# A fused attention and gated-convolution kernel: the softmax exchange from tile 6, queries and keys turned in blocks from tile 7 and fetched with four tokens per partition, and a new order of the opening

## The chip, the core and the metric

The kernel runs on one core of one Trainium2 chip. A core has a matrix engine (TensorE, PE in the rows; its weight loads are PEld), a vector engine (VectorE, DVE), a scalar engine (ScalarE, ACT), a general engine (GpSimd, POOL) and a sequencer that issues DMAs (SyncE, SP). The five run side by side, each works through its own queue in order, and they wait for each other by semaphores. The metric is the time on the device in microseconds (us); shorter is better.

## The reference

Two stages, in fp32. There are 8 sequences of 576 tokens, 8 heads of 64, a model width of 512 and a hidden width of 1024.

```python
scores = q @ k.T / sqrt(64) - slope[head] * |i - j|     # masked to 0 <= i - j < 128
attn = exp(scores - max) / (sum + 1e-9)                 # over the keys
x = concat over heads of attn @ v                       # (8, 576, 512)
h = relu(x @ w_in)                                      # (8, 576, 1024)
conv_out[s] = w[0]*h[s-1] + w[1]*h[s] + w[2]*h[s+1]     # per channel, zeros outside the sequence
out = (h * sigmoid(conv_out)) @ w_out                   # (8, 576, 512)
```

## The kernel before

**Tiles, chunks, steps.** The 8 x 576 tokens are one row of 4608, cut into 36 attention tiles of 128 tokens. A query tile sees its own 128 keys and the 128 before, so both tiles' scores go into one buffer and a predicated copy chooses by position. Sequence boundaries fall at multiples of 576, that is on a tile edge at tiles 9, 18 and 27, and in the middle of tiles 4, 13, 22 and 31. The second stage works in 18 chunks of 256 tokens, each in 4 steps of 256 hidden channels: step s belongs to chunk s // 4.

**The order.** It is written by hand as strings of pieces. `OPENING` (lines 862 to 892) runs once, `PERIOD` 14 times (two tiles and four steps in each), `TAIL` once. Each piece is a letter code with a tile (or step) and sometimes a half; it issues its instructions at the end of the queues of its engines, so the string is the order on every engine at once, and pieces near each other in it are meant to run at about the same time. The pieces that matter here, by engine:

- PE: `QU` transposes queries and keys of half a tile (4 transposes; `Q` is a whole tile, 8), `S` scores, `T` transposes the softmax of half a tile (4), `AV` softmax times values, `UH` step s's up-projection (8 matmuls in fp32 for steps 0 to 3, 12 later), `D` its down-projection.
- DVE: `MP` and `MB` mask and add the bias, `TQ` block transpose of queries and keys, `TE` block transpose of the softmax, `CA`/`CB` the outer taps of the convolution, `GT` the gate, `V` the bits of a weight block, `XF` copies one column of the ring that holds the attention output x.
- ACT: `QV` copies transposed queries and keys out of PSUM, `HQ` rounds block-turned ones to the matmul's type, `X` exponentials, `Z`, `TH`, `HH`, `GH` of the second stage.
- POOL: `CL`, `SG` on weight blocks, `SEL`/`CE` cut the softmax by position, `GL` the low part of the gate.
- Either of two engines, by sets at lines 155 to 161: `W` the low part of a weight block, `LQ` the low part of queries and keys, `N` the normalising, `RS` a scaling of a weight block.
- SP: `LD`, `LV` loads of queries and keys and of values, `F` weight blocks, `WE`/`SE` the exchange, and the output.

**Two ways for queries and keys.** Matmuls contract over partitions, so queries and keys must be turned. Up to tile 8 (`t < TURN`, 9) they are loaded with one token per partition, transposed on PE and copied by ACT; tiles 7 and 8 have their low parts from `QM` and `QL` on DVE, and the keys of tile 6 are converted for tile 7 by `KH`, `KL` and `KT`. From tile 9 each DMA brings 32 tokens of 4 heads (`load_blocks`, 16 DMAs a tile), and DVE transposes in blocks of 32 by 32:

```python
nc.sync.dma_start(out=dst[:, g, (r + m) // BK],
                  in_=src[b, g * NB : (g + 1) * NB, s + m : s + m + BK, :])
```

`HQ` and `LQ` then read the block in the order in which it lies, 1024 values a partition in one instruction each.

**Two ways for the softmax.** Before tile 8 (`t < FIRST`) PE transposes it (`T`), ACT copies it (`RL`), POOL cuts it (`SEL`), and `AV` has 32 matmul records with 128 rows. From tile 8 DVE transposes blocks (`TE`), SP writes them to DRAM (`WE`) and reads them back with the blocks exchanged (`SE`), POOL cuts them (`CE`), and `AV` has 64 records with 64 rows, whose two halves are summed by `XA` (ACT) and `XS` (DVE); `XL`, the low part of x, is on POOL there and on DVE before.

**Where the stages meet.** The first up-projection in the long form, `UH4.0`, reads x of tiles 2 and 3 and one column of tile 4, which `XF4` on DVE has to put in place.

## Time and profile before

| what | value |
|---|---|
| median of 3 runs (lowest, highest) | 570.08 us (568.88, 571.22) |
| the profiled execution's own time | 568.98 us |
| its span, first to last instruction | 567.3 us |
| PE busy | 558.1 us, 98% of the span |
| DVE busy | 463.2 us, 82% |
| ACT busy | 430.6 us, 76% |
| POOL busy | 394.8 us, 70% |
| mean granted clock of PE | 0.997 |

Busy time is the time in which an engine has an instruction running, overlaps counted once. It is an average over stages with different limits, so the rows below go by stretches of the opening. Matmuls are pipelined: what a group of them costs PE is the distance from its start to the start of the next group, not the printed duration, which holds the last one's way through the array.

### The profile page before, as it was taken

The page shows a single profiled execution, that of the slowest core. Times are in us where ns is not written, and L with a number is a line of the kernel's source. Part 1 is how long each engine was busy: PE and PEld are TensorE (multiplying, and loading weights), DVE is VectorE, ACT ScalarE, POOL GpSimd, SP SyncE. Part 2 cuts the span into 40 slices and gives each one's busy share as a digit, 9 for nine tenths or more (in the row PEclk, how much of TensorE's full clock was granted, in tenths as well). Part 3 has the DMA queues.
Part 4 walks back from the last instruction along what each step waited for, and adds up shares of the span by engine and source line. Part 5 has one row for each costly group of instructions (what it writes and reads, how often), then busy time and mean ns, then how long its engine had stood idle before and what let it go on. Part 6 is the DMA issues. An engine that isn't in the chain of part 4 may idle for free.

```text
span 567.3 us, 16990 instructions
## 1 busy us (share of the span) xinstructions
PE 558.1 (98%) x6121; PEld 490.0 (86%) x6121; DVE 463.2 (82%) x1474; ACT 430.6 (76%) x1225; POOL 394.8 (70%) x453
## 2 busy tenths in 40 slices
...
GB/s 196 260 251 138 258 36 76 99 70 160 134 156 139 131 164 125 175 121 173 124 177 124 172 125 174 125 175 125 174 123 171 125 171 79 150 112 25 16 11 66
DMA packets 141225, 76.63 MB, mean 135 GB/s; under 512 B 116412, under 2 KB 131028, under 8 KB 141140
## 3 DMA queue, kind: packets, MB, share of 16 engines
...
q8 instruction: 48, 0.79, 0.6%
q14 instruction: 37, 0.30, 0.2%
...
## 4 chain that ended last, share of the span: by engine, by line
PE 91%; DVE 4%; DMA 2%; issue 1%; SPq 1%; ACT 0%; DVEq 0%
PE o L801 34%; PE p L698 34%; PE sc L387 8%; PE av L592 7%; PE o L791 2%; DMA rqk<-in_k_dram 2%; PE sc L432 2%; DVE sc L458 1%; PE av L632 1%; PE p L693 1%; SPq L320 1%; DVE wg L216 1%; PE pt L330 1%; DVE e L476 1%; DVE low L209 0%
## 5 line engine op out<-in xcount | busy, mean ns | idle before, releaser
L698 PE MATMUL p<-ring,wi 128*128 128x256 f32 x1088 | 195.4, 281 | 0.0
L731 DVE SCALAR_TENSOR_TENSOR zp<-hh,cw,zp 128x256 f32<-128x256 f32 (+7 forms) x384 | 160.5, 418 | 41.5 <-ACT zp L716 34.0
L698 PEld LDWEIGHTS p<-ring,wi 128*128 128x128 f32 x1088 | 168.7, 188 | 3.3 <-issue 0.2
L698 PE MATMUL p<-ring,wl 128*128 128x256 f32 x544 | 152.3, 280 | 0.0
L767 POOL TENSOR_TENSOR gl<-z,gh 128x512 fp32r<-128x512 f32 x67 | 86.8, 1296 | 79.9 <-ACT gh L758 79.1
L484 ACT ACTIVATE e<-e,st 128x128 f32<-128x128 f32 x288 | 112.7, 394 | 17.7 <-DVE st L476 17.4
L801 PE MATMUL o<-wo,gh 128*128 128x512 f32 x270 | 110.3, 409 | 0.0
L801 PE MATMUL o<-wo,gl 128*128 128x512 f32 x270 | 105.7, 392 | 0.0
L801 PE MATMUL o<-wl,gh 128*128 128x512 f32 x270 | 105.6, 391 | 0.0
L698 PEld LDWEIGHTS p<-ring,wl 128*128 128x128 f32 x544 | 102.7, 189 | 0.0
L716 ACT ACTIVATE zp<-hh,cw 128x256 f32<-128x256 f32 x144 | 68.9, 478 | 30.8 <-DVE z L746 20.2
L508 POOL TENSOR_TENSOR e<-e,st 128x512 f32<-128x512 f32 x60 | 62.4, 1041 | 15.1 <-DVE st L496 14.9
L368 POOL TENSOR_TENSOR qkT_low<-blk,qkT 128x1024 fp32r<-128x1024 f32 x25 | 59.9, 2397 | 16.8 <-ACT qkT L361 10.5
L476 DVE CUSTOM_DVE_ANT_0 e<-sc,bias 128x128 f32<-128x128 f32 x288 | 69.0, 285 | 1.1 <-DVE sc L458 0.2
L738 ACT ACTIVATE zp<-zp 128x512 f32<-128x512 f32 (+1 forms) x73 | 42.1, 577 | 33.3 <-DVE zp L731 33.1
L801 PEld LDWEIGHTS o<-wo,gh 128*128 128x128 f32 x270 | 50.6, 187 | 13.8 <-issue 0.2
L746 DVE SCALAR_TENSOR_TENSOR z<-zp,hh 128x512 f32<-128x512 f32 (+1 forms) x73 | 49.3, 676 | 14.1 <-ACT zp L738 12.3
L801 PEld LDWEIGHTS o<-wo,gl 128*128 128x128 f32 x270 | 50.6, 187 | 11.6
L710 ACT ACTIVATE hh<-p 128x512 f32<-128x512 f32 x67 | 40.0, 597 | 26.2 <-PE p L698 24.1
L801 PEld LDWEIGHTS o<-wl,gh 128*128 128x128 f32 x270 | 50.8, 188 | 9.5
L458 DVE COPY_PREDICATED sc<-m_prev,sc 128x256 f32<-128x256 uint8 x128 | 50.9, 420 | 8.9 <-PE sc L387 6.4
L484 ACT ACTIVATION_READ_ACCUMULATOR e<-e,st 128x1 f32 x288 | 54.3, 188 | 0.0
...
## 6 DMA issues: line engine op xcount, KB each, us to landing
...
```

What stands on the lines that cost most here:

```text
L368: eng.tensor_tensor(out=turned_of(qkT_low, t), in0=blks[t], in1=hi, op=ALU.subtract)
L387: nc.tensor.matmul(to, turned_of(tq, t)[rows, 0, g, b], of, start=n == 0, stop=n == len(passes) - 1)
L458: nc.vector.copy_predicated(out=s_cur, mask=mask.unsqueeze(1).to_broadcast(shp), data=data)
L476: nc.vector.tensor_tensor_reduce(out=e[:, j, :], in0=s_cur[:, g, :], in1=bias[:, head_of(t, u * HU + j), :], scale=-0.125, scalar=FAR, op0 ...
L484: nc.scalar.activation(out=e[:, j, :], in_=e[:, j, :], func=AF.Exp, bias=st[:, 0, j : j + 1], scale=-1.0, accum_out=st[:, 1, j : j + 1],)
L508: eng.tensor_tensor(out=e, in0=e, in1=st[:, 2, :].unsqueeze(2).to_broadcast([P, HU, P]), op=ALU.mult)
L698: nc.tensor.matmul(ps, a[:, part], ring[:, i, cc, cols], start=cc == 0 and n == 0, stop=cc == NCC - 1 and n == 2)
L716: nc.scalar.activation(out=zps[s][:, ff, :], in_=hhs[s][:, ff, 1 : 1 + CW], func=AF.Copy, scale=cw[:, 1, f : f + 1])
L731: nc.vector.scalar_tensor_tensor(out=z[:, ff, a:cut], in0=hh[:, ff, a + kk : cut + kk], scalar=cw[:, kk, f : f + 1], in1=z[:, ff, a:cut], ...
L746: nc.vector.scalar_tensor_tensor(out=zgs[s][:, ff], in0=zps[s][:, ff], scalar=1.0, in1=hhs[s][:, ff, 1 : 1 + CW], op0=ALU.add, op1=ALU.mult,)
L767: eng.tensor_tensor(out=gl, in0=zgs.pop(s), in1=as32(gh), op=ALU.subtract)
L801: nc.tensor.matmul(to, a[:, ff, ms], w[:, part], start=first and n == 0, stop=end and n == 2)
```

## The change

- `EXCH = 6`: the exchange by blocks (`TE`, `WE`, `SE`, `CE`, `AV` in quarters, `XA`, `XS`, `XL` on POOL) is used from tile 6 on instead of tile 8.
- `TURN = 7`: queries and keys are turned by blocks from tile 7 on instead of tile 9. Tile 7 also needs the keys of tile 6 in this form, so they are loaded and turned a second time, with tile 7. `QM`, `QL`, `QO`, `Q`, `KH`, `KL` and `KT` are gone; up to tile 6 the scores have one pass.
- `load_blocks`: each partition receives four tokens next to each other (1 KB) instead of one. A whole tile takes 4 DMAs (2 for queries, 2 for keys) instead of 16. A tile with a sequence boundary in its middle (13, 22, 31) takes 32 of 16 partitions each, instead of 16 of 128.
- A turned block now holds its tokens in the order of the four-token groups. `HQ` and `LQ` put them back in order as they read: the innermost dimension of the read is 4 values, 128 bytes apart. Each is now two instructions of 512 values a partition (queries, keys), and three for tile 7.
- Other engines for some pieces: `LQ9` and `LQ10` go from DVE to POOL (and `LQ7`, `LQ8` exist on POOL), `GL4` and `GL8` from POOL to DVE, one `W` and several `N` and `RS` change engine.
- `OPENING` is written anew. `PERIOD` and `TAIL` are the same strings.

The core of the diff:

```diff
+    EXCH = 6
+    TURN = 7
...
-    LOW_POOL = {2, 3, 7, 8, 9, 10, 11, 13, 14, 16}
-    RB_POOL = {0, 1, 3, 4, 5, 7, 9, 15}
-    N_ACT = {(1, 0), (2, 0), (3, 0), (4, 0), (4, 1), (5, 0), (5, 1)}
-    N_POOL = {(6, 0), (6, 1), (7, 0), (7, 1), (8, 0), (8, 1), (9, 0), (9, 1), (10, 0), (10, 1)}
-    GL_DVE = set()
-    KL_POOL = {(6, 0)}
-    LQ_DVE = {9, 10}
+    LOW_POOL = {1, 6, 7, 8, 10, 11, 12, 13, 14, 15, 16}
+    RB_POOL = {0, 3, 5, 8, 15}
+    N_ACT = {(1, 1), (2, 0), (3, 0), (4, 0), (4, 1), (5, 0), (5, 1), (7, 0), (9, 0), (9, 1)}
+    N_POOL = {(6, 0), (6, 1), (8, 0), (8, 1), (10, 0), (10, 1)}
+    GL_DVE = {4, 8}
+    LQ_DVE = set()
...
-                for m in range(0, n, BK):
-                    nc.sync.dma_start(
-                        out=dst[:, g, (r + m) // BK],
-                        in_=src[b, g * NB : (g + 1) * NB, s + m : s + m + BK, :],
-                    )
+                of = src[b, g * NB : (g + 1) * NB, s : s + n, :].rearrange("h (p m) d -> h p (m d)", m=NB)
+                if n == P:
+                    nc.sync.dma_start(out=dst[:, g].rearrange("p m d -> p (m d)"), in_=of)
+                    continue
+                for h in range(NB):
+                    rows = slice(h * BK + r // NB, h * BK + (r + n) // NB)
+                    nc.sync.dma_start(out=dst[rows, g].rearrange("p m d -> p (m d)"), in_=of[h])
...
+            if t == TURN:
+                raws[t, "k"] = apool.tile([P, NG, NB, D], F32, name=f"rk{t - 1}", tag="rqk", bufs=3)
+                load_blocks(t - 1, raws[t, "k"], k)
...
+    def by_token(blk):
+        return blk.rearrange("p g b (m c) -> p (g b) c m", c=BK)
+
+    def in_order(x):
+        return x.rearrange("p g b (c m) -> p (g b) c m", m=NB)
...
-        nc.scalar.copy(out=turned_of(qkT_of(t), t), in_=blks[t])
+        if t == TURN:
+            nc.scalar.copy(out=in_order(turned_of(qkT_of(t), t - 1)[:, 1]), in_=by_token(blks[t, "k"]))
+        for i in range(2):
+            nc.scalar.copy(out=in_order(turned_of(qkT_of(t), t)[:, i]), in_=by_token(blks[t][:, i]))
...
-        eng.tensor_tensor(out=turned_of(qkT_low, t), in0=blks[t], in1=hi, op=ALU.subtract)
+        for i in range(2):
+            eng.tensor_tensor(
+                out=in_order(turned_of(qkT_low, t)[:, i]), in0=by_token(blks[t][:, i]), in1=in_order(hi[:, i]),
+                op=ALU.subtract,
+            )
...
-        eng = nc.gpsimd if t > TURN + 1 or (t, u) in N_POOL else nc.vector
+        eng = nc.gpsimd if t > FIRST + 2 or (t, u) in N_POOL else nc.vector
...
-            eng = nc.vector if t <= FIRST else nc.gpsimd
+            eng = nc.vector if t < EXCH else nc.gpsimd
```

`t < FIRST` and `t >= FIRST` become `t < EXCH` and `t >= EXCH` in `turn_e`, `write_e`, `swap_e`, `select_e`, `av`, `x_part`, `x_sum`, `x_hi` and `x_lo`. The new opening, from the scores of tile 6 to the second up-projection in the long form, and its end:

```
S6.1 MP6.1.1 MP6.1.0 MB6.1.0 X5.1.1 S6.0 MB6.1.1
MP6.0.0 Z0.1 CA0.1 MB6.0.0 SEL3.0 CB0.1 W5 AV3 X5.1.0 CL9 SG12 SEL4.0 RL4.1 SEL4.1 AV4 TH0 TQ7 X5.0.1 NR5 F15 GT0
RS9 SG9 XH3 X6.1.1 CL11 Z1.0 W2 HQ7 CL16 LQ7 XH4 CA1.0 V12 UH3.0 HH3.0 H7 CB1.0 XL4 F13 W3 H6 Z1.1 UH3.1 HH3.1
CA1.1 CB1.1 UH2.0 N5.1 UH2.1 CL13 XL3 TH1 GT1 W6 XF4 T5.1 H8 MP6.0.1 W7 HH2.0 Z2.0 HH2.1 CA2.0 CB2.0 Z2.1 MB6.0.1
X6.0.0 CA2.1 RS11 UH4.0 SG11 LD9 F14 CB2.1 RL5.1 V9 RS13 SG13 TH2 LD8 GT2 GL2 V11 X6.0.1 GL0 UH4.1 N6.0 Z3.0
...
TH7 GT7 H12 H16 HH8 W14 Z8.0 W12 TE8.1 WE8 GL6 MB9.0.0 X9.0.0 W13 SE7 CA8.0 GH7 GL7 CB8.0 Z8.1 X9.1.1 X9.1.0
CA8.1 CB8.1 TH8 GT8 UH10.1 UH10.0 W16 S10.0 MP10.0.1 X9.0.1 N9.0 MP10.1.0 SE8 D5 D6 MB10.1.0 MP10.1.1 CE7.0 CE7.1
LD11 CE8.0 Z9.0 TE9.0 N9.1 CA9.0 CB9.0 CE8.1 Z9.1 MB10.1.1 CA9.1 CB9.1 X10.1.0 X10.1.1 TH9 MP10.0.0 TE9.1 WE9 GH8
GL8 D7 OB7 GT9 N10.1
```

## Rows read from the trace of the kernel before

**Rows 1.** The page's first part: busy us, share of the span, instructions.
```profile
PE 558.1 (98%) x6121; PEld 490.0 (86%) x6121; DVE 463.2 (82%) x1474; ACT 430.6 (76%) x1225; POOL 394.8 (70%) x453
```

**Rows 2.** Busy time by stretch: length, busy us of each engine (instructions), clock, DMA.
```profile
4.00:30.00 26.00, 23.70 (x180) 18.21 (x179) 21.03 (x99) 21.69 (x84) 13.05 (x20) 0.93 1.01 240
30.00:52.00 22.00, 20.12 (x161) 15.80 (x160) 21.12 (x62) 21.46 (x72) 14.35 (x20) 1.00 0.94 229
52.00:66.00 14.00, 13.71 (x119) 11.40 (x119) 13.28 (x39) 11.96 (x38) 10.53 (x15) 1.00 0.61 195
66.00:126.00 60.00, 59.96 (x492) 48.34 (x491) 56.35 (x161) 48.84 (x147) 44.30 (x52) 1.00 0.34 87
```

**Rows 3.** Chain that ended last, merged pieces: start us, us, engine, tile, line, count.
```profile
128.62 1.90 PE av L632 x32
134.97 1.62 PE sc L387 x44
186.79 2.84 PE av L592 x128
```

**Rows 4.** Timeline of PE, 19 to 32 us: start, us, instruction, [idle before <-releaser].
```profile
23.74 0.41 PE L330 MATMUL pt<-ident_r,rqk 128*128 128x128 f32 x2 [1.06 <-DMA rqk<-in_k_dram]
```

**Rows 5.** Timeline of PE, 60 to 95 us: groups whose start-to-start distances are prices.
```profile
72.27 0.39 PE L432 MATMUL sc<-qkT 64*128 64x256 f32 x2
...
73.88 3.70 PE L791 MATMUL o<-wg,z 128*128 128x512 f32 x8
...
81.29 1.04 PE L514 MATMUL pa<-ident_r,e 128*128 128x128 f32 x8
82.08 0.48 PE L698 MATMUL p<-ring,wi 128*128 128x256 f32 x2
...
85.00 1.04 PE L330 MATMUL pt<-ident_r,rqk 128*128 128x128 f32 x8
85.80 0.48 PE L698 MATMUL p<-ring,wi 128*128 128x256 f32 x2
...
88.83 3.71 PE L632 MATMUL av<-rl,rv 128*64 128x128 f32 x64
```

**Rows 6.** Groups by line and shape, 0 to 180 us, DVE: count | busy us, mean ns.
```profile
L348 DVE STREAM_TRANSPOSE blk<-rqk 128x1024 f32<-128x1024 f32 x6 | 7.4, 1238 | 0.2 <-DMA rqk<-in_k_dram 0.2
L746 DVE SCALAR_TENSOR_TENSOR z<-zp,hh 128x512 f32<-128x512 f32 x17 | 11.6, 681 | 1.4 <-ACT zp L738 1.2
L731 DVE SCALAR_TENSOR_TENSOR zp<-hh,cw,zp 128x256 f32<-128x256 f32 x48 | 23.2, 483 | 1.3 <-ACT zp L716 0.5
L235 DVE TENSOR_TENSOR wl<-wg,wi 128x512 fp32r<-128x512 f32 x4 | 3.6, 904 | 0.0
L341 DVE TENSOR_TENSOR qkT_low<-pt,qkT 128x512 fp32r<-128x512 f32 x4 | 2.6, 676 | 0.0
```

**Rows 7.** Timeline of DVE, 62 to 67 us: the copy of `XF4`.
```profile
65.43 0.18 DVE L666 CAST ring<-ring 128x8 fp32r<-128x8 f32 x1
```

**Rows 8.** Timeline of PE, 60 to 95 us: `UH4.0`, the first up-projection in the long form.
```profile
66.31 0.59 PE L698 MATMUL p<-ring,wi 128*128 128x256 f32 x2
```

**Rows 9.** Timeline of SP, 100 to 185 us: queries of tile 13, then the exchange's reads.
```profile
129.33 4.85 SPq L285 DMA_DIRECT2D rqk<-in_q_dram  x8
...
139.33 4.74 SPq L561 DMA_DIRECT2D rr<-scr  x8
```

**Rows 10.** Groups by line and shape, 0 to 180 us, POOL: one operand, two operands.
```profile
L767 POOL TENSOR_TENSOR gl<-z,gh 128x512 fp32r<-128x512 f32 x12 | 15.9, 1322 | 7.9 <-ACT gh L758 7.8
L177 POOL TENSOR_SCALAR wst<-wst 128x512 f32<-128x512 f32 x16 | 11.6, 722 | 13.2 <-DMA wst<-in_moe_w_in_dram 12.2 <-DMA wst<-in_moe_w_out_dram 0.8
```

**Rows 11.** Timelines of POOL and PE in the second period: `LQ13`, `XL9`, `XL10`, then `S13`.
```profile
159.43 2.39 POOL L368 TENSOR_TENSOR qkT_low<-blk,qkT 128x1024 fp32r<-128x1024 f32 x1 [0.30 <-ACT qkT L361]
...
162.76 2.56 POOL L658 TENSOR_TENSOR ring<-xx,ring 128x512 fp32r<-128x512 f32 x2
...
163.47 0.39 PE L387 MATMUL sc<-qkT 32*128 32x256 f32 x4
```

More of the change, by code (lines that the diff above doesn't have):

```diff
@@ L252, in qkT_of @@
     def qkT_of(t):
-        kind = F32 if t < SPLIT else F32R
+        kind = F32 if t < TURN else F32R
         if kind not in qkTs:
@@ L334, in qkT_out @@
         to = qkT_of(t)[:, t % SLOTS, u]
[L335 removed]
+        ps = pts.pop((t, u))
         nc.scalar.copy(out=to, in_=ps)
[L338 to L341 removed]
     def turn(t):
@@ L345, in turn @@
             return
-        assert TURN * P % S == 0
+        if t == TURN:
+            blks[t, "k"] = apool.tile([P, NG, D // BK, P], F32, name="blk_k", tag="rl", bufs=4)
+            nc.vector.transpose(
+                out=blks[t, "k"].rearrange("p g b (m c) -> p g m b c", c=BK),
+                in_=raws[t, "k"].rearrange("p g m (b r) -> p g m b r", r=BK),
+            )
         blks[t] = apool.tile([P, 2, NG, D // BK, P], F32, name="blk", tag="rl", bufs=4)
@@ L391, in scores_blocks @@
             sms[t, u] = pss[2 * u : 2 * u + 2]
-    def keys_hi(t, u):
-        nc.scalar.copy(out=qkT_low[:, t % SLOTS, u, 0], in_=qkT_of(t)[:, t % SLOTS, u, 1])
-    def keys_low(t, u):
-        hi, low = (qkT_low[:, t % SLOTS, u, i] for i in range(2))
-        eng = nc.gpsimd if (t, u) in KL_POOL else nc.vector
-        eng.tensor_tensor(out=low, in0=qkT_of(t)[:, t % SLOTS, u, 1], in1=as32(hi), op=ALU.subtract)
-    def keys_top(t, u):
-        nc.scalar.copy(out=qkT_of(t + 1)[:, t % SLOTS, u, 1], in_=as32(qkT_low[:, t % SLOTS, u, 0]))
     def window(t):
@@ L424, in scores @@
         top = qkT_of(t)
-        passes = ((top, top),) if t < SPLIT else ((top, top), (top, qkT_low), (qkT_low, top))
         for g in range(NG):
-            for n, (tq, tk) in enumerate(passes):
-                for a in range(2):
-                    rows = slice(a * D, (a + 1) * D)
-                    to = pss[a][:, g] if first else pss[a][:, g, cur]
-                    of = tk[rows, keys, u, 1, g, :] if first else tk[rows, slot, u, 1, g, :]
-                    nc.tensor.matmul(
-                        to, tq[rows, slot, u, 0, g, :], of, start=n == 0, stop=n == len(passes) - 1
-                    )
+            for a in range(2):
+                rows = slice(a * D, (a + 1) * D)
+                to = pss[a][:, g] if first else pss[a][:, g, cur]
+                of = top[rows, keys, u, 1, g, :] if first else top[rows, slot, u, 1, g, :]
+                nc.tensor.matmul(to, top[rows, slot, u, 0, g, :], of, start=True, stop=True)
         sms[t, u] = pss
@@ L601, in x_sum @@
     def x_sum(t):
-        if t < FIRST:
+        if t < EXCH:
             return
@@ L874, in tile_alibi_window_attention_conv_glu @@
-    HH0.0 H5 W5 RS6 F9 S5.0 H3 MP5.0.1 MB5.0.1 QV6.0 SG6 V6 T4.0 RL4.0 SEL4.0 X5.1.0 F12 CL12 UH0.1 HH0.1 SEL3.0 T4.1
-    RL4.1 S6.0 MP6.0.0 MB6.0.0 MP5.0.0 LV4 H1 X5.1.1 X5.0.1 MP6.0.1 W1 Z0.0 QU6.1 QV6.1 KH6.1 UH3.0 UH2.0 H7 SEL4.1
-    MB5.0.0 KH6.0 X5.0.0 CA0.0 CB0.0 HH2.0 SEL3.1 S6.1 MP6.1.0 Z0.1 CA0.1 CL9 AV3 KL6.1 HH3.0 RS12 SG12 H6 CB0.1
-    MB6.1.0 TH0 AV4 MB6.0.1 GT0 V12 XH3 X6.1.0 KL6.0 GL0 NR5 XH4 XL4 LD7 QU7.1 QV7.1 QM7.1 UH3.1 Z1.0 N5.1 HH3.1 XL3
-    LV6 QU7.0 LD11 W2 F11 CL11 QV7.0 CA1.0 CB1.0 W3 Z1.1 H8 KT6.0 T5.1 RS9 SG9 XF4 RL5.1 F14 MP6.1.1 UH2.1 UH4.0
```

83 lines of the change are left out of this document (36 added, 47 removed).

## The prediction, made before the kernel ran

> **What bounds the kernel now.** I read the busy shares first: PE has work on it for 98% of the span, no other engine for more than 82% [rows 1]. The reader is to see that time is won only where PE gets less to do or waits less. The chain that ended last says the same of the steady part: from the second period on it is PE from group to group. So the table by stretches comes next, for the opening, which is all that the change rewrites. From 4 to 30 us PE is idle for 26.0 - 23.7 = 2.3 us, from 30 to 52 for 1.9, from 52 to 66 for 0.3, and from 66 to 126 for nothing [rows 2]. In the two early stretches VectorE (21.0 of 26, 21.1 of 22) and ScalarE (21.7 and 21.5) are nearly full, and the first loads hold PE too: the transposes of tile 4 wait 1.06 us for their keys [rows 4]. The opening is thus in two parts: up to about 66 us VectorE, ScalarE and DMA set the pace, and from `UH4.0` at 66.31 [rows 8] PE runs without a gap to the end. The gate between them is x in the ring, finished by `XF4` at 65.43 [rows 7].
>
> **What it takes off PE.** Distances from start to start:
> - Softmax transposes `T` of tiles 6 and 7: 16 transposes; 8 take 82.08 - 81.29 = 0.79 us [rows 5], so 1.6 us.
> - Query and key transposes of tiles 7 and 8: 8 take 85.80 - 85.00 = 0.80 [rows 5], so 1.6 for both, of which tile 8's 0.8 lies behind `UH4.0` and tile 7's before it.
> - `AV` of tiles 6 and 7 in quarters: 2.84 / 2 = 1.42 a tile [rows 3] for 3.71 / 2 = 1.85 [rows 5] and 1.90 [rows 3]: 0.9 less.
> - Scores of tiles 7 and 8: three passes on 64 rows took 73.88 - 72.27 = 1.61 us [rows 5], the blocked form on 32 rows 1.62 [rows 3]: nothing.
>
> That is 4.1 us in all, 3.3 of it behind `UH4.0`, where PE has no gap and each us less is a us of the span if nothing else becomes late. The 0.8 before it only lets PE arrive earlier.
>
> **What it puts before `UH4.0`.** Comparing the two strings up to `XF4`, VectorE gets the block transpose of tile 7 (1.24) and of tile 6's keys, half as large (0.62), `W2` and `W3` (2 x 0.90), `GT1` (0.68), `CA1.1` and `CB1.1` (2 x 0.48): 5.3 us. It loses `QM7.1` (0.68), `W1` (0.90) and `KL6.1` (0.34, a half of `QM`'s size): 1.9 [rows 6]. The rest swaps like for like. That leaves 3.4, or about 3.0 because the instructions overlap: `XF4` is shown for 0.18 us, but its successor starts 0.09 after it. So `XF4` is between 65.4 (all of the 3.0 goes into gaps that VectorE has now: 5.0 + 0.9 + 0.7 = 6.6 us from 4 to 66 [rows 2], a part of it before the first scores are there) and 68.4 (none does). I take half, 66.9, since the gaps are not all at the place where the new work stands. `UH4.0` then starts at 67.1 instead of 66.3: 0.8 later, and -0.7 to +2.3 by the two ends.
>
> **Loads.** Each tile's queries and keys need 4 issues instead of 16; at 4.85 / 8 = 0.6 us an issue [rows 9] SP gets 7 us free per tile. In the steady part no PE wait is ended by such a load, so that is worth nothing; in the opening it lets weights be fetched sooner, which no PE gap behind 66 us asks for. But tiles 13, 22 and 31 need 32 issues, some 19 us instead of 10. For 13 and 31 the exchange's write and reads stand right behind them in SP's queue, the reads now at 139.33 [rows 9]; they move about 9 us back. POOL cuts what they bring, and behind the cuts it has `N`, `LQ` and `XL`, on which the next period's scores and up-projections wait. The next `AV` comes about 157.7 (two periods lie between 128.62 and 186.79 [rows 3], so 29.1 each). From 139.33 that is 18.4 us, of which the issues take 4.7 [rows 9] and four cuts at about 0.72 (a one-operand row of this size [rows 10]) 2.9; of the 10.8 left, 9 go, and 1.8 remain for the landing. I count 0.3 us for each of two tiles, 0.6 in all, between 0 and 2.6 (1.3 each).
>
> **Strided reads.** `HQ` and `LQ` read words 128 bytes apart. No row shows such a read. `LQ` of 1024 values took 2.39 us [rows 11]; two of 512 are 2 x 1.32 = 2.6 unslowed [rows 10], the lower end. The upper end: as if the strided operand cost as much as one operand more, that is 1.32 - 0.72 = 0.6 for 512 [rows 10], so 3.8. After `LQ13` POOL has ended at 161.82, and `S13`, which needs it, starts at 163.47 [rows 11]: 1.65 us in hand, for 0.2 to 1.4 more. `XL10`, behind it on POOL, ends at 165.32, and PE turns to its reader only after the scores and a down-projection. I take 2.6 to 3.2, near the two-operand row, and so count nothing. `HQ` in two instructions adds about 0.1 us on ScalarE, which has room behind 66 us (48.8 of 60 [rows 2]).
>
> The Trainium skill, "GPSIMD Engine Reference", section "Performance pitfalls for Q7 kernels", says that a read with more than 8 bytes from element to element costs about half as much again per element. By it the pair would be an estimated 3.9 us, just inside the 1.65 in hand, so the sum stays, with the cover used up. No row here shows such a read, so the trace neither agrees nor differs.
>
> **Other engines behind 66 us.** POOL takes over `LQ8` to `LQ10` (3 x 2.6) and `XL6` (1.3) and gives up `GL4`, `GL8` and some `N`: about +2 to +6 on 44.3 us in a stretch of 57 [rows 2]; hidden, at no cost. A new wait: the cuts of tiles 6 and 7 now wait on POOL for a round trip through DRAM, and `LQ8` (for the scores of tile 8) and `GL` are queued behind them; with POOL a quarter idle I count 0, and what it costs if that fails stands in the second rival. VectorE has 56.35 of 60 there [rows 2] and gets about 2.7 us more up to `TE8.1` (softmax transposes of tiles 6 and 7, another of queries and keys, `GL4`; `QM`, `QL` and two `LQ` go); I count nothing and price it in that rival too.
>
> **The sum.** -3.3 + 0.8 + 0.6 = -1.9. From the profiled execution's 568.98 us that is 567.1; this execution was 1.1 below the median of the runs, so the median to expect is 570.08 - 1.9 = 568.2 us.
>
> **Rivals.**
> 1. *All of PE's credit shows.* If the new order fills VectorE's gaps, `UH4.0` comes at 65.6 (PE itself could be there, having 0.8 less to do), and -3.3 - 0.7 = -4.0 gives 566.1; fewer waits in the first 52 us, where PE idles 4.2 [rows 2], could carry it to 564. For it: the gaps are there. Against it: VectorE was at 96% from 30 to 52 us, and tile 4's load still lands no earlier.
> 2. *VectorE paces the whole opening.* None of the 3.0 is absorbed, then the further 2.7 isn't either: `TE8.1` is 5.6 us later, and write, read and cut of tile 8 stand between it and `AV8`, the first period's second `AV`. `UH4.0` at 68.6 alone leaves -1.0; PE's wait at the exchange adds 0 to 5. I price it at 571, 569.5 to 574. For it: 56.35 of 60. Against it: PE had no gap there while VectorE was that full.
> 3. *Slower: the strided `LQ` comes after the scores that need it, in every period.* It decides from a pair of 2.39 + 1.65 = 4.0 us on; each us beyond costs a us in each of 14 periods. At 4.5, 14 x 0.5 = 7 us: 575. For it: reads with such a step are in no row. Against it: the upper end from the rows is 3.8, and `HQ` in halves lets the first `LQ` start sooner. It needs a price above both my ends. By the rule of the Trainium skill above, 3.9, it would stop just short.
>
> That the change doesn't do what it says would be seen in a `QU` or `T` left on PE for tiles 7 on; the diff leaves none.
>
> **How the numbers follow.** The forecast 0.40 (own range 566.0 to 570.5), rival 1 0.26 (564 to 567.2), rival 2 0.22 (569.5 to 574), rival 3 0.12. A measurement can tell a change of 0.5%, 2.85 us, so faster is below 567.2 and slower above 572.9. Faster: rival 1 and a third of the forecast, 0.40. Slower: rival 3 and a quarter of rival 2, 0.18. Within: 0.42. The range 564.2 to 573.5 leaves out most of rival 3 and the ends of the others, under 2 in 10.
>
> **What would show it.** PE has 16 softmax transposes and 16 of queries and keys less. `XF4` near 66.9 and `UH4.0` near 67.1; a start before 65.8 speaks for rival 1, after 68.3 for rival 2. From there to `AV7` in the first period, now 128.62 - 66.31 = 62.3 us [rows 3, 8], 2.8 less, 59.5, without a gap (the rest of the 3.3 is `AV7` itself). `LQ` pairs under 4.0 us, no wait of the scores on POOL, periods of 29 us. After tiles 13 and 31 at most about 1 us of wait at `AV` or the scores. I am wrong if periods grow, or if PE has gaps between `UH4.0` and the first period.

## The result, and the profile after

The changed kernel took 578.06 us (median of 4 runs, 577.2 to 579.56) beside 569.48 us for the kernel before on the same chip (4 runs, 568.01 to 571.22): a ratio of 1.015, 95% interval 1.0117 to 1.0182. It is slower, where I had forecast 568.2 with a range up to 573.5.

The page's first part for the kernel after, columns as in [rows 1]: ScalarE is busy 33.7 us longer over the whole span, GpSimd 26.4, VectorE 2.8, and TensorE, which was to get less, 1.4.

```profile
PE 559.5 (97%) x6201; PEld 490.2 (85%) x6201; DVE 466.0 (81%) x1475; ACT 464.3 (81%) x1262; POOL 421.2 (73%) x481
```

The same stretches as in [rows 2], kernel after:

```profile
4.00:30.00 26.00, 23.49 (x176) 18.06 (x175) 21.06 (x95) 21.78 (x83) 12.54 (x19) 1.00 1.05 249
30.00:52.00 22.00, 19.65 (x158) 15.76 (x158) 21.37 (x64) 19.88 (x65) 13.71 (x19) 1.00 0.77 212
52.00:66.00 14.00, 10.39 (x102) 8.14 (x100) 13.44 (x37) 12.36 (x37) 11.63 (x14) 1.00 0.58 193
66.00:126.00 60.00, 56.63 (x534) 45.10 (x535) 54.90 (x149) 52.12 (x147) 47.59 (x50) 0.97 0.41 118
```

The first 52 us are little changed. From 52 to 66 us TensorE is now idle for 3.6 us instead of 0.3, and from 66 to 126 for 3.4 instead of none. A marker tells how much later the opening ends: the first period begins with the up-projection `UH11.1`. TensorE's timeline, kernel before and kernel after:

```profile
125.63 0.40 PE L698 MATMUL p<-ring,wi 128*128 128x256 f32 x2
```
```profile
131.99 0.40 PE L706 MATMUL p<-ring,wi 128*128 128x256 f32 x2
```

So the opening ends 6.4 us later. 4.8 of them are there at `UH4.0` already (71.12 below, 66.31 in [rows 8]); the stretch from it to the first period took 60.9 us instead of 59.3. From the first period to the start of the tail it was 400.2 us before and 403.5 after; 3.2 of this lie in three periods, the third, sixth and twelfth (30.35, 29.73 and 29.80 us instead of 29.06, 28.55 and 29.06). These two, 6.4 and 3.4, are the loss (the tail was 0.4 shorter); the profiled execution took 578.32 us, 9.3 more than the one before.

**Where TensorE waits in the opening.** Its timeline, kernel after (in brackets the idle time before the row, and what ended it):

```profile
55.53 1.13 PE L442 MATMUL sc<-qkT 64*128 64x256 f32 x8 [1.90 <-ACT qkT L340]
...
66.37 3.76 PE L701 MATMUL p<-x_first,wg 128*128 128x258 f32 x16 [1.80 <-ACT hh L714]
...
71.12 0.51 PE L706 MATMUL p<-ring,wi 128*128 128x256 f32 x2 [0.56 <-DVE ring L674]
...
96.24 0.86 PE L410 MATMUL sc<-qkT 32*128 32x256 f32 x2 [0.37 <-ACT hh L718]
98.85 0.56 PE L410 MATMUL sc<-qkT 32*128 32x256 f32 x2 [1.75 <-DVE ring L668]
```

`UH4.0` starts at 71.12, 4.8 us later than in [rows 8]; it waited for `XF4`. The scores of tile 8 (96.24) stop in the middle until `HH6` and `XL5` have emptied buffers in PSUM, the memory that TensorE writes to. What those waits hang on is seen in ScalarE's queue, where the strided `HQ` stands in front of them (timeline of ScalarE, kernel after):

```profile
62.40 1.14 ACT L372 CAST qkT<-blk_k 128x512 fp32r<-128x512 f32 x1
63.42 2.13 ACT L374 CAST qkT<-blk 128x512 fp32r<-128x512 f32 x2
65.43 0.61 ACT L659 CAST ring<-av 128x512 fp32r<-128x512 f32 x1
65.91 0.41 ACT L714 ACTIVATE hh<-p 128x258 f32<-128x258 f32 x1
...
93.52 2.17 ACT L374 CAST qkT<-blk 128x512 fp32r<-128x512 f32 x2
95.56 1.10 ACT L718 ACTIVATE hh<-p 128x512 f32<-128x512 f32 x2
```

`HQ7` holds ScalarE from 62.40 to 65.55. `XH4` (65.43), without which neither `XL4` nor `XF4` can go, and `HH3.0` (65.91), for which TensorE waits, stand behind it. `HQ8` does the same to `HH7` and `HH6` at 95.56. For `XF4` ScalarE was not the only late one: VectorE, which does `XL4`, `XL3` and `XF4`, worked without a wait from 62.51 to 69.35, and in the run below in which `HQ` reads in lying order `UH4.0` came only 0.6 us earlier.

The wait at 96 us has a second price. Busy time by stretch, columns as in [rows 2]:

```profile
88.00:96.00 8.00, 7.87 (x134) 7.43 (x133) 7.89 (x15) 6.02 (x15) 5.91 (x6) 1.00 0.37 99
96.00:98.80 2.80, 0.76 (x2) 0.36 (x2) 1.98 (x4) 2.80 (x8) 2.80 (x5) 1.00 0.80 180
98.80:102.80 4.00, 3.95 (x48) 3.31 (x49) 3.54 (x8) 3.92 (x6) 2.49 (x2) 0.57 0.28 96
```

After TensorE had been busy for only 0.76 of 2.8 us, the clock granted to it was 0.57 for the next 4 us, mostly the lower of its two levels (1.2 of 2.4 GHz). At full clock the 3.95 busy us would be 4.00 x 0.57 = 2.3, so the wait of 2.1 us (0.37 and 1.75) cost 1.7 more.

**What the other engines have more.** Busy time from the start to the first period, kernel before and kernel after:

```profile
0.00:125.63 125.63, 119.97 (x956) 96.22 (x956) 114.01 (x373) 104.86 (x334) 83.36 (x112) 0.99 0.62 156
```
```profile
0.00:131.99 131.99, 118.99 (x1004) 94.79 (x1004) 118.79 (x378) 112.78 (x347) 92.68 (x116) 0.99 0.61 166
```

VectorE has 4.8 us more, ScalarE 7.9, GpSimd 9.3. Up to `UH4.0` it is 5.0, 3.7 and 4.8 us more, behind it -0.2, 4.2 and 4.6. For ScalarE the row that grew is `HQ`, for GpSimd `LQ` (groups by shape, kernel after: count | busy us, mean ns):

```profile
L374 ACT CAST qkT<-blk 128x512 fp32r<-128x512 f32 x58 | 63.2, 1138 | 0.1
```
```profile
L388 POOL TENSOR_TENSOR qkT_low<-blk,qkT 128x512 fp32r<-128x512 f32 x58 | 91.2, 1593 | 19.4 <-ACT qkT L374 19.4
```

VectorE's instructions are 378 instead of 373. On balance most of what grew is the time of instructions that it had before. The shifts of weight blocks (`V`), in the opening, kernel before and after:

```profile
L216 DVE SCALAR_TENSOR_TENSOR wg<-wg,wst 128x512 uint32<-128x512 uint32 x10 | 8.7, 868 | 0.4
L209 DVE SCALAR_TENSOR_TENSOR wst<-wst 128x512 uint32<-128x512 uint32 x9 | 6.2, 686 | 0.0
L209 DVE SCALAR_TENSOR_TENSOR low<-wst 128x512 uint32<-128x512 uint32 x6 | 4.9, 820 | 0.0
```
```profile
L217 DVE SCALAR_TENSOR_TENSOR wg<-wg,wst 128x512 uint32<-128x512 uint32 x10 | 10.2, 1023 | 0.4
L210 DVE SCALAR_TENSOR_TENSOR wst<-wst 128x512 uint32<-128x512 uint32 x9 | 6.9, 762 | 0.0
L210 DVE SCALAR_TENSOR_TENSOR low<-wst 128x512 uint32<-128x512 uint32 x6 | 5.9, 978 | 0.0
...
L674 DVE CAST ring<-ring 128x8 fp32r<-128x8 f32 x1 | 0.8, 764 | 0.0
```

That is 23.0 - 19.8 = 3.2 us more for the same 25 instructions, and the small copy `XF4` took 764 ns where it had taken 180 [rows 7]. GpSimd was at work beside it (`W6`), and beside the shifts of `V12` too (`LQ7`, 63.6 to 69.2). Beside the copy of before GpSimd was at work as well, but with an instruction that ended at 65.58, 0.15 us after the copy had begun; `W6`'s first ended at 71.03, 0.72 us after, and each copy ended within 0.04 us of it (65.61 and 71.07).

**In the periods.** The largest single wait of a period belongs to tile 22, which crosses a sequence boundary. Timelines of SP and of VectorE, kernel after:

```profile
265.87 10.36 SPq L289 DMA_DIRECT2D rqk<-in_q_dram  x16
276.27 8.53 SPq L289 DMA_DIRECT2D rqk<-in_k_dram  x16
```
```profile
286.14 1.25 DVE L352 STREAM_TRANSPOSE blk<-rqk 128x1024 f32<-128x1024 f32 x1 [4.12 <-DMA rqk<-in_k_dram]
...
287.37 0.65 DVE L614 TENSOR_TENSOR xx<-xx,av 128x512 f32<-128x512 f32 x1
```

The 32 issues end at 284.8, `TQ22` stands first in VectorE's queue and waits 4.12 us, and `XS` behind it, which frees PSUM for the next scores, comes late.

### The profile page after: what moved, and what is told of

It is laid out like the page before. It is cut to its first block, busy times and chain, and to the rows that moved or that the text cites. A ratio compares the mean times of both kernels' runs of the same rounds, so it can differ in the third digit from the quotient of the medians.

```text
span 576.6 us, 16956 instructions
## 1 busy us (share of the span) xinstructions
PE 559.5 (97%) x6201; PEld 490.2 (85%) x6201; DVE 466.0 (81%) x1475; ACT 464.3 (81%) x1262; POOL 421.2 (73%) x481
## 4 chain that ended last, share of the span: by engine, by line
PE 75%; DVE 10%; ACT 6%; SPq 4%; DMA 3%; issue 1%; DVEq 0%; ACTq 0%
PE o L809 30%; PE p L706 27%; PE sc L410 7%; PE av L600 6%; SPq L289 3%; DVE sc L466 2%; DMA rqk<-in_k_dram 2%; ACT e L492 1%; DVE zp L739 1%; PE o L799 1%; DVE e L484 1%; DMA scr<-eb 1%; ACT qkT L374 1%; PE sc L442 1%; PE idle L72 1%
## 5 line engine op out<-in xcount | busy, mean ns | idle before, releaser
L775 POOL TENSOR_TENSOR gl<-z,gh 128x512 fp32r<-128x512 f32 x65 | 84.0, 1292 | 60.8 <-ACT gh L766 56.1
L388 POOL TENSOR_TENSOR qkT_low<-blk,qkT 128x512 fp32r<-128x512 f32 x58 | 91.2, 1593 | 19.4 <-ACT qkT L374 19.4
L516 POOL TENSOR_TENSOR e<-e,st 128x512 f32<-128x512 f32 x56 | 58.4, 1043 | 11.9 <-DVE st L504 11.9
L374 ACT CAST qkT<-blk 128x512 fp32r<-128x512 f32 x58 | 63.2, 1138 | 0.1
L809 PEld LDWEIGHTS o<-wo,gh 128*128 128x128 f32 x270 | 50.6, 187 | 13.7 <-issue 0.2
```

The source lines that it names most:

```text
L374: nc.scalar.copy(out=in_order(turned_of(qkT_of(t), t)[:, i]), in_=by_token(blks[t][:, i]))
L388: eng.tensor_tensor(out=in_order(turned_of(qkT_low, t)[:, i]), in0=by_token(blks[t][:, i]), in1=in_order(hi[:, i]), op=ALU.subtract,)
L516: eng.tensor_tensor(out=e, in0=e, in1=st[:, 2, :].unsqueeze(2).to_broadcast([P, HU, P]), op=ALU.mult)
L775: eng.tensor_tensor(out=gl, in0=zgs.pop(s), in1=as32(gh), op=ALU.subtract)
L809: nc.tensor.matmul(to, a[:, ff, ms], w[:, part], start=first and n == 0, stop=end and n == 2)
```

## The experiments

My theory from these rows was that the strided reads on ScalarE, the 32 issues and the fuller queues of the opening are separate costs. The first eight runs take parts away or do one part alone. "P0" is the start of `UH11.1`.

**Reads in lying order.** The kernel after, with

```diff
 def by_token(blk):
-    return blk.rearrange("p g b (m c) -> p (g b) c m", c=BK)
+    return blk.rearrange("p g b k -> p (g b) k")
 def in_order(x):
-    return x.rearrange("p g b (c m) -> p (g b) c m", m=NB)
+    return x.rearrange("p g b k -> p (g b) k")
```

> The changed kernel (578.1 us) with HQ and LQ reading the turned block in the order in which it lies, so no read is strided; the tokens of a tile from 7 on then stand in the order of their groups of four, and the values that come out are those of other token pairs. Everything else stays: loads, exchange, order, the two instructions of 512. Theory A (the strided reads on ScalarE and GpSimd cost the time): HQ falls from 1.14 to about 0.6 us an instruction, LQ from 1.59 to 1.3, and the time to 568-571. Theory B (the new order with its exchange and its four-buffer scores from tile 7 costs it): HQ and LQ get shorter all the same, but the time stays at 575-578.

574.48 us (574.1 to 575.15), ratio to before 1.0091 [1.0064, 1.0118]; P0 at 129.31. The same two rows in this kernel:

```profile
L374 ACT CAST qkT<-blk 128x512 fp32r<-128x512 f32 x58 | 32.6, 610 | 0.0
```
```profile
L388 POOL TENSOR_TENSOR qkT_low<-blk,qkT 128x512 fp32r<-128x512 f32 x58 | 74.9, 1314 | 8.0 <-ACT qkT L374 7.9
```

The step costs ScalarE 1138 / 610 = 1.87 times and GpSimd 1.21 times. It is worth 3.6 us, 2.7 of them in the opening. That lies between the ranges of the two theories: the step is a part of the loss and does not explain the rest.

**The old loads in the new order.** The edit above, and `load_blocks` as before the change (16 DMAs a tile, one token per partition).

> The changed kernel with the loads of the kernel before (16 DMAs a tile, one token a partition) and with it the packed HQ and LQ reads; it computes the reference. Theory A: as with packed reads alone, 568-571, since no wait in the steady part hangs on a load. Theory B: 575-578. If the quick loads were what the new opening lives on, this one is over 2 us slower than the one with four-token loads and packed reads.

578.2 us (576.85 to 580.69), ratio 1.016 [1.0121, 1.0199]; P0 at 134.99. Against the run with packed reads the four-token loads are worth 3.7 us in the new order: they pay for the strides and no more.

**No crossing tiles.** The kernel after; tiles 13, 22 and 31 fetch neighbouring tokens (other data) with 4 DMAs:

```diff
 for r, b, s, n in segments(t):
+    if n < P:
+        if r:
+            continue
+        s, n = S - P, P
```

> The changed kernel, but tiles 13, 22 and 31 fetch 128 neighbouring tokens of one sequence with 4 DMAs instead of their own with 32 (other data, same work). Theory C (the 32 issues delay the exchange): the periods that are longer than before, the third (30.4), sixth (29.7) and twelfth (29.8), come back to 29.1 or less, and the time is 575.0, 3 less. If the strided LQ makes these waits, nothing changes: 577-579.

576.76 us (574.79 to 578.62), ratio 1.0134 [1.009, 1.0177]. P0 131.6 as in the kernel after, P0 to tail 401.3 instead of 403.5, and VectorE's wait for `rqk` (8.3 us in three) gone. Theory C had 575.0; by the times the gain is 1.3 us, and the two intervals overlap. The periods say more: the third, sixth and twelfth took 29.76, 28.55 and 29.57 us, 2.0 less together than in the kernel after. The sixth, in which tile 22 is turned, took 28.55 us in each of the seven kernels of this document that load it as before or with 4 DMAs, and 29.03 to 32.11 in the eleven that load it with 32. The crossing loads cost about 2 us.

**The step on VectorE instead.** The block transpose writes in token order, 16 bytes apart, and `HQ` and `LQ` read as it lies.

```diff
-    out=blks[t].rearrange("p i g b (m c) -> p (i g) m b c", c=BK),
+    out=blks[t].rearrange("p i g b (c m) -> p (i g) m b c", m=NB),
```

> The changed kernel with the reordering moved into the block transpose on VectorE, which writes its words 16 bytes apart in the order of the tokens; HQ and LQ read packed. It computes the reference. Theory A: 568-571 if the transpose still takes 1.2 us; if the strided write doubles it to 2.4, VectorE gets 1.2 us more a tile, 572-576 in the opening's stalls. Theory B: 575-578.

580.17 us (577.88 to 581.45), ratio 1.0185 [1.0146, 1.0224]. That is above every range named, and the step is no cheaper on VectorE. The transpose took 2062 ns instead of 1238:

```profile
L352 DVE STREAM_TRANSPOSE blk<-rqk 128x1024 f32<-128x1024 f32 x29 | 59.8, 2062 | 7.4 <-DMA rqk<-in_k_dram 7.4
```

**Parts alone, in the order of before.** Four kernels put pieces of the change into the old string at the places of what they replace: the whole change; the exchange from tile 6 alone (`EXCH = 6`); the turned queries and keys from tile 7 alone (`TURN = 7`, with four-token loads and strided reads; it pairs the heads of tile 7 in another order); the loads and strided reads alone, from tile 9.

> All of the change except the order: the changed kernel's code (exchange from tile 6, turn from 7, four-token loads, strided reads) in the opening of the kernel before, with its sets of engines; the pieces that went are taken out, and TE, WE, SE, CE, XA, XS, TQ, HQ, LQ stand where T, RL, SEL, QU, QV, QM stood. Theory D (the new order costs what is left beside the strides): the credit of 4.1 us shows less the 3.6 of the strides and about 2 of the 32-issue loads: 569-572. Theory E (the parts themselves make waits, whatever the order): 575-580.

> The kernel before with the exchange from tile 6 as its only change, in its own opening. Theory D: PE loses 16 transposes and 0.9 us of AV, 2.5 us in all, and 566.5-568.5 come out. Theory E: the round trip through DRAM makes POOL and PE wait in the opening, 571-575.

> The kernel before with turned queries and keys from tile 7, four-token loads and strided reads, in its own opening, the exchange from tile 8 as before. Theory D: 1.6 us of transposes less, 3 to 5 of strides and 32-issue loads more: 570.5-573. Theory E: VectorE and ScalarE have no room for TQ7, HQ7 and TQ8, HQ8 in the opening, 574-578.

> The kernel before with four-token loads and strided HQ and LQ reads alone, turn from tile 9, exchange from tile 8, its own opening. By the changed kernel's periods, which took 3.4 us more in sum, 569.1 + 3.4 + 0.5 = 573. If the strides and the 32 issues cost only in the crowded new opening, 569-570.

| part | time, us (range) | ratio to before | P0 |
|---|---|---|---|
| all, old order | 591.38 (590.15 to 592.06) | 1.0397 [1.0376, 1.0418] | 146.8 |
| exchange from 6 | 578.44 (576.75 to 580.15) | 1.0178 [1.0144, 1.0211] | 134.6 |
| turned from 7 | 585.4 (583.13 to 588.01) | 1.0295 [1.026, 1.0331] | 136.5 |
| loads and strides only | 574.93 (572.27 to 576.79) | 1.0106 [1.0068, 1.0144] | 126.0 |

Each part alone is slower, the first three by more than either theory had. The new order gives back some 13 of the 22.4 us that the whole change costs in the old one (591.38 against 568.98 for the kernel before on that chip). The pieces were not fitted to the old order any further, so these are upper prices. They also hold time that TensorE lost at the lower of its two clock levels after its waits: up to P0 the mean granted clock was 0.93 in the first of the four (0.99 in the kernel before). The last line changes no order: its loss is in the periods (P0 to tail 407.5 us, 7.3 more), 3.6 of it in the period of tile 22. Of these 3.6, one wait of TensorE took 1.76 us, and a granted clock of 0.50 for 3.4 us behind it cost up to 1.7.

**Which stepped read.** The next four ask what holds the opening. Only `HQ` in lying order:

```diff
-    nc.scalar.copy(out=in_order(turned_of(qkT_of(t), t)[:, i]), in_=by_token(blks[t][:, i]))
+    nc.scalar.copy(out=turned_of(qkT_of(t), t)[:, i], in_=blks[t][:, i])
```

> Only ScalarE's copies of the turned queries and keys read and write in lying order (tokens of the first operand come out permuted, so the values differ); GpSimd's subtractions stay strided, loads and order are those of the kernel after. Theory A (ScalarE's stepped read, 1138 against 610 ns per 512 elements, stands ahead of the steps that free TensorE's PSUM buffers): most of the 2.7 us that packed reads gave in the opening comes from here; first period starts at 129 to 130 us instead of 132.0, time 575 to 576 us. Rival B (GpSimd's stepped subtraction, 1593 against 1314 ns, is what TensorE waits for): first period stays at 131.5 to 132, time 577.5 to 578.5.

575.56 us (573.56 to 578.46), ratio 1.0093 [1.0063, 1.0123]; P0 at 128.93, `UH4.0` at 70.52. All of the 2.7 us comes from ScalarE; GpSimd's step costs the opening nothing that shows. Of the 3.1 us 0.6 are there at `UH4.0`; the other 2.5 come behind it, where TensorE's granted clock was 1.00 in this run and 0.97 in the kernel after.

**Moved pieces.** The kernel after with `UH3`, `UH2`, their `HH`, `XH4`, `XL4`, `XL3`, `XF4`, `D2`, `AV5`, `XH5` and `XL5` earlier:

```diff
-... S6.0 ... AV4 TH0 TQ7 ... XH3 X6.1.1 ... HQ7 ... XH4 CA1.0 V12 UH3.0 HH3.0 ... XL4 ... UH3.1 HH3.1 ... UH2.0 ... XF4 ...
+... UH3.0 S6.0 ... HH3.0 ... AV4 UH3.1 UH2.0 UH2.1 TH0 TQ7 ... XH3 XH4 X6.1.1 ... HH3.1 HQ7 ... CA1.0 XL4 XL3 XF4 V12 ...
-... HH6 TQ9 H13 Z5.1 CA5.1 AV5 XH5 XL5 CB5.1 AV6 XA6 XS6 N7.1 S8.0 ... D2 ...
+... HH6 TQ9 AV5 XH5 XL5 H13 Z5.1 CA5.1 CB5.1 AV6 XA6 XS6 N7.1 D2 S8.0 ...
```

> The kernel after with a few pieces of the opening moved: UH3.0 between the two scores of tile 6 and HH3.0 behind it, UH3.1, UH2.0, UH2.1 straight after AV4, XH4, XL4, XL3 and XF4 ahead of V12 and of HQ7, HH3.1 ahead of HQ7, D2 ahead of S8, XH5 and XL5 ahead of H13 and Z5.1. Theory A (the late opening is a matter of a few places in the order: 3.6 us of idle TensorE between 52 and 66 us and 2.2 us in the scores of tile 8): UH4.0 starts at 67 to 68 instead of 71.1, first period at 127 to 129 instead of 132.0, time 573 to 575.5 us. Rival B (VectorE, ScalarE and GpSimd have too much work for this opening in any order, so a wait that is moved comes back before its end): UH4.0 earlier, but the first period at 131 or later, time 577 or more.

580.48 us (580.17 to 580.91), ratio 1.017 [1.013, 1.021]; P0 at 132.74. The idle places were filled, and a wait came back at another. TensorE's timeline in this kernel:

```profile
61.16 5.50 PE L701 MATMUL p<-x_first,wg 128*128 128x258 f32 x24
70.16 1.35 PE L522 MATMUL pa<-ident_r,e 128*128 128x128 f32 x4 [3.49 <-ACT e L513]
71.16 0.78 PE L706 MATMUL p<-ring,wi 128*128 128x256 f32 x2
```

TensorE had done its up-projections by 66.7, then waited 3.49 us for the normalised softmax of tile 5, which ScalarE reached at 69.72. In front of it stood `HQ7` and, last, a wait for VectorE, which had `V12` and `CB1.0` to do first (timeline of ScalarE in this kernel):

```profile
69.30 0.48 ACT L724 ACTIVATE zp<-hh,cw 128x256 f32<-128x256 f32 x1 [1.00 <-DVE zp L739]
69.72 1.26 ACT L513 ACTIVATE e<-e,st 128x128 f32<-128x128 f32 x4
```

`UH4.0` started at 71.16, as in the kernel after. These moves are not the few places that theory A looked for. That no other order would do is not shown by one set of moves.

**Both.**

> Both: the moved pieces of the order, and all reads of the turned queries and keys in lying order (tokens permuted, so the values differ). Theory A (order and stepped reads are separate causes): the gains add, first period at 125 to 126.5, time 570 to 572. Rival B (both take away the same wait): first period at 128 to 129.5, time 573 to 574.5.

576.99 us (576.28 to 578.4), ratio 1.0111 [1.0069, 1.0154], P0 at 132.0: no faster than the packed reads without the moves (1.0091, in overlapping intervals; P0 129.31). Neither theory had it; the moves are no gain with either form of reading.

**The exchange of tiles 6 and 7 taken back,** with packed reads, `T`, `RL` and `SEL` at the places of `TE` and `CE`:

```diff
-    EXCH = 6
+    EXCH = 8
```

> The kernel with all reads in lying order (574.5 us), with the softmax exchange from tile 8 as before, so that tiles 6 and 7 are transposed on TensorE again (heads of tile 7 are paired in another order, and tokens are permuted, so the values differ). TensorE gets 2.5 us of work back (transposes 1.6, quarters 0.9). Theory A (the exchange of tiles 6 and 7 costs nothing beside TensorE): 576 to 577.5, first period at 131 to 132. Rival B (its turning on VectorE, its two dozen transfers and its selection on GpSimd cost the opening more than TensorE saves): 574 or less, first period at 129 or earlier.

580.23 us (578.65 to 582.6), ratio 1.0168 [1.0119, 1.0218], P0 at 136.6. It lost 5.7 us, more than TensorE's 2.5, and lies outside both ranges. So at these places the earlier exchange does pay, and it is not what holds the opening; the old pieces were not fitted to the new order.

**Added work, one engine at a time.** The last four settle what "has room" was worth. The kernel before, six times four operations that nobody reads, on VectorE, ScalarE or GpSimd:

```diff
+def more_work(n):
+    for i in range(n):
+        nc.vector.tensor_tensor(out=junk, in0=bias[:, i, :], in1=bias[:, 4 + i, :], op=ALU.add)
```

(`nc.scalar.copy(out=junk, in_=bias[:, i, :])` and `nc.gpsimd.tensor_tensor` in the other two.)

> The kernel before, with 24 additions of 128x128 on VectorE that nobody reads, four each after GT0, CA1.1, GT1, GT2, GT3 and GT4: 4.8 us at an estimated 0.2 us, as much as VectorE is busier in the opening of the kernel after (118.8 against 114.0 us). Theory A (the opening goes by VectorE's amount of work): first period at 129 to 131 instead of 125.6, time 572.5 to 575. Rival B (VectorE has room there, as my prediction had it): first period at 127 or earlier, time 570.5 or less.

> The kernel before, with 24 copies of 128x128 on ScalarE that nobody reads, four each after TH0, Z1.1, TH1, TH3, TH4 and TH5: 7.7 us at 0.32 us, as much as ScalarE is busier in the opening of the kernel after (112.8 against 104.9 us). Theory A (VectorE's work alone sets the opening, ScalarE at 83% has room): first period at 127 or earlier, time 570.5 or less. Rival B (any work of ScalarE ahead of the steps that free TensorE's buffers counts): first period at 129 to 132, time 572.5 to 575.5.

> The kernel before, with 24 additions of 128x128 on GpSimd that nobody reads, at the places where the other run put VectorE's: an estimated 0.38 us each (half of 0.73 for 128x256), 9 us, as much as GpSimd is busier in the opening of the kernel after. VectorE gets no instruction more. Theory A (VectorE's instructions with SBUF operands wait while a GpSimd instruction runs, as the 24 additions did: 290 ns beside an idle GpSimd, 1085 beside a busy one): VectorE is busy 2 to 5 us longer in the opening and the first period starts at 127.5 to 131, time 571.5 to 575. Rival B (GpSimd has room, 66% in the opening, and its work hurts nobody): first period at 126.5 or earlier, VectorE's busy time within 1 us, time 570 or less.

What the additions themselves took, in the three kernels:

```profile
L838 DVE TENSOR_TENSOR junk<-bias 128x128 f32<-128x128 f32 x24 | 13.7, 571 | 0.6
```
```profile
L838 ACT COPY junk<-bias 128x128 f32<-128x128 f32 x24 | 7.1, 296 | 0.6
```
```profile
L838 POOL TENSOR_TENSOR junk<-bias 128x128 f32<-128x128 f32 x24 | 12.0, 502 | 1.5
```

| added to | busy us added | P0 later by | time, us (range) | ratio |
|---|---|---|---|---|
| VectorE | 13.7 | 13.9 | 582.38 (581.75 to 582.91) | 1.0228 [1.02, 1.0256] |
| ScalarE | 7.1 | 3.4 | 573.73 (572.51 to 575.79) | 1.009 [1.0061, 1.012] |
| GpSimd | 12.0 | 5.3 | 575.85 (574.31 to 579.37) | 1.0112 [1.0053, 1.017] |

For every us on VectorE the opening ends 1.0 us later, for one on ScalarE or GpSimd nearly half a us (0.48 and 0.44), although TensorE was hardly idle there in the kernel before [rows 2]. A part of this is TensorE's clock. In the run with VectorE's additions it fell to the lower level twice, first after TensorE had been busy for 4.11 of 5.9 us (columns as in [rows 2]):

```profile
65.90:69.30 3.40, 3.40 (x9) 2.64 (x9) 3.12 (x13) 1.94 (x6) 1.14 (x2) 0.50 1.18 307
103.40:110.20 6.80, 5.98 (x16) 3.19 (x17) 6.70 (x21) 4.96 (x14) 2.15 (x2) 0.50 0.39 84
```

At full clock these 9.4 busy us would be 4.7, so up to 4.7 of the 13.9 us are the clock; with GpSimd's additions it is up to 1.7 of 5.3 (0.50 for 3.4 us from 77.0), with ScalarE's nothing behind 30 us. That VectorE has room is refuted even so (9.2 for 13.7), and so is that VectorE alone counts. My sizes for an addition were low (0.2 us on VectorE and 0.38 on GpSimd, where 0.57 and 0.50 came); on VectorE that is mostly the stretch beside GpSimd. VectorE's additions in the first of these kernels, and GpSimd beside them:

```profile
L838 DVE TENSOR_TENSOR junk<-bias x24: 280/292/1421, 59.7 to 100.8; 128x128 f32<-128x128 f32 x24
```
```profile
70.40 3.69 DVE L838 TENSOR_TENSOR junk<-bias 128x128 f32<-128x128 f32 x4
...
79.12 1.26 DVE L838 TENSOR_TENSOR junk<-bias 128x128 f32<-128x128 f32 x4
```
```profile
70.70 1.29 POOL L235 TENSOR_TENSOR wl<-wg,wi 128x512 fp32r<-128x512 f32 x1
71.96 0.69 POOL L177 TENSOR_SCALAR wst<-wst 128x512 f32<-128x512 f32 x1
72.61 1.34 POOL L235 TENSOR_TENSOR wl<-wg,wi 128x512 fp32r<-128x512 f32 x1
...
80.61 1.04 POOL L508 TENSOR_TENSOR e<-e,st 128x512 f32<-128x512 f32 x1 [5.38 <-DVE st L496]
```

Min, median and max of one are 280, 292 and 1421 ns. Four took 1.26 us while GpSimd stood idle (79 us) and 3.69 while it worked (70 us); the 11 that met no GpSimd work took 290 ns on average, the 8 that lay beside it 1085. `CA` and `MB`, which read PSUM, show no such stretch. The Trainium skill, "SBUF — State Buffer", section "SBUF: two separate sides", says that VectorE and GpSimd share one pair of ports, locked for the whole of an instruction, and that a VectorE instruction with two SBUF inputs needs it against a GpSimd instruction that reads SBUF; the trace agrees. With GpSimd's additions, though, VectorE was busy only 1.4 us longer up to P0 (115.4 against 114.0), below the 2 to 5 that the theory wanted. The time, 575.85, is 0.85 above that theory's range as well. Most of the slip came down GpSimd's own queue and ScalarE's, as the scores of tile 7 waiting 2.94 us for `HH`:

```profile
76.88 0.50 PE L432 MATMUL sc<-qkT 64*128 64x256 f32 x1 [2.94 <-ACT hh L710]
```

In the same execution the periods took 3.0 us more than before (P0 to tail 403.2), though nothing was added to them; the tenth to twelfth hold it. A difference of 3 us in the periods of one execution alone can thus be chance.

**VectorE's work taken off.** The kernel with only `HQ` packed, without `CB` of steps 1 to 5 in the opening's string.

> The kernel with only ScalarE's copies in lying order (575.6 us), without the second side of the convolution (CB) of steps 1 to 5: ten VectorE instructions of 0.49 us, 4.9 us less (one tap of the convolution is left out there, so the values differ). Theory A (VectorE's amount of work sets the opening): first period at 124.5 to 126 instead of 128.9, time 571 to 573. Rival B (ScalarE, GpSimd and the waits between engines set it): first period at 127.5 or later, time 574 or more.

571.58 us (570.09 to 572.77), ratio 1.0033 [1.0014, 1.0053], from 1.0093: 3.4 us less for 3.8 us less of VectorE (114.7 against 118.5). P0 moved only from 128.93 to 127.40, a tenth short of where the rival has it, and P0 to tail from 403.0 to 401.5. The time is as VectorE's amount of work would have it, but the place is not; why the periods gained (the second 1.0 us, the sixth 0.6) is open, and chance is one answer. For the opening the run says less than it seems: of the ten instructions only two stand before `XF4`, and `UH4.0` came 0.6 us earlier for them (69.90 after 70.52).

## Why the prediction was wrong

- **The step that failed is the cover: "I take half" of VectorE's 3.0 us before `UH4.0`, "ScalarE, which has room", and with them every edit in the opening costed at nothing because another engine hides it.** VectorE's busy time from the start to the end of `XF4`, kernel before and kernel after (columns as in [rows 2]):

```profile
0.00:65.61 65.61, 59.99 (x467) 47.92 (x468) 57.68 (x214) 56.00 (x190) 39.09 (x61) 0.97 0.87 218
```
```profile
0.00:71.07 71.07, 60.57 (x463) 48.27 (x463) 63.14 (x218) 60.33 (x196) 44.44 (x63) 1.00 0.80 211
```

VectorE was busy for 5.5 us more and idle for 7.9 us in both, so on balance none of the added work went into its gaps. The 3.0 was too small as well: about 2.6 of the 5.5 are shifts (`V`) and `XF4` itself taking longer than before. `UH4.0` came 4.8 us later where 0.8 was forecast.
- **`HQ`** in two instructions was priced at 0.1 us. A pair took 2.13 to 2.34 us instead of one instruction of 1.04, nine such instructions stand in the opening, 9 x 0.53 = 4.8 us, and taking the step away brought the opening 3.1 us forward, 2.5 of it behind `UH4.0`.
- **The sizes of the other engines' work behind `UH4.0`** are not what failed: "+2 to +6" on GpSimd was 4.6, "about 2.7" on VectorE was -0.2. What failed is that they are hidden. The shares that I read as room (48.8 of 60, and 44.3 of 57, where [rows 2] has 60) tell how busy an engine is, not whether somebody waits for its next instruction: an added us cost 0.48 on ScalarE, 0.44 on GpSimd and 1.0 on VectorE, the clock's part included. GpSimd's 4.8 us before `UH4.0` were not in the sum at all.
- **"From `UH4.0` PE runs without a gap" was a fact of the kernel before that I used as a property of the stage.** A TensorE without gaps in a hand-made order says that the others arrive just in time. Taking 0.8 + 2.8 = 3.6 us off TensorE before the first period gave nothing that shows, and VectorE, busy for 114 of the 125.6 us before, got more to do and not less. The two signs that I named came true: gaps between `UH4.0` and the first period, and periods that grow.
- **`XF4` and `UH4.0`:** 66.9 and 67.1 were forecast, 68.4 was my upper end for `XF4`, 70.3 and 71.1 came. I had counted VectorE's instructions and left out that `V12` and `XF4` stretch beside `LQ7` and `W6`. That `XH4` stands behind `HQ7` on ScalarE I left out too, but it is worth little here (the 0.6 us above).
- **The loads:** 0.6 us was forecast for tiles 13 and 31 and nothing, without a reason, for 22; together they cost about 2, more than half of it in the period of tile 22 (29.73 and 28.55). I looked for the damage at the exchange's reads behind the issues. It came at the first reader, `TQ22`, which blocks VectorE's queue.
- **What held:** `LQ` pairs stayed under 4.0 us (3.03 to 3.92, on average 2 x 1.59 = 3.2, the forecast's upper end), and no score waits of any length were for `LQ`, so the third rival did not decide. The rule on strided reads that I cited from the Trainium skill, "GPSIMD Engine Reference", section "Performance pitfalls for Q7 kernels", half as much again, is above what was measured, 21% for an instruction with one strided and one more operand.
- **The second rival** had the right kind of cause and the right sign (`UH4.0` after 68.3), and it had VectorE's 3.0 us wholly unabsorbed, as measured. At 571 it lacked ScalarE's reads, the stretch of VectorE beside GpSimd, and the loads; its further 2.7 us on VectorE behind `UH4.0` (3.0 and 2.7 are 5.7, not 5.6) did not come.

Of the loss, 6.4 us in the opening and 3.4 in the periods, runs that took a part away explain these, each by one profiled execution: in the periods the crossing loads about 2 and the steps 1.5; in the opening ScalarE's step 3.1. What remains is 3.3 us of the opening: the kernel with `HQ` packed still begins its first period that much late, although TensorE has less to do. All of it stands before `UH4.0`, which comes 4.2 us late there; from `UH4.0` to the first period that kernel took 58.4 us, 0.9 less than the kernel before. VectorE's 5.0 us more of busy time up to `UH4.0` are enough for the 4.2. That they are the cause is argued from the equal idle time and not shown by a run that takes them away. How much of it is VectorE's added work and how much its stretch beside GpSimd stays open.

No version that was run beats the kernel before.
